# Block attention and a feed-forward product: weight scales by blocks, from sums of squares, with each weight tile fetched once

## The chip, the cores and the metric

The kernel runs on one core of a Trainium2 chip. The metric is the device time of one execution in microseconds, the median of several runs. A core has five engines that run side by side and wait for one another by semaphores: TensorE (PE, and PEld for its weight loads), VectorE (DVE), ScalarE (ACT), GpSimd (POOL) and SyncE (SP), which here issues all transfers.

## The reference

```python
def _attn_ref(q, k, v):                     # (4, 8, 768, 64) each
    block, window = (32, 16)
    k_sum = k.reshape(B, H, nb, block, D).max(axis=3)
    v_sum = v.reshape(B, H, nb, block, D).mean(axis=3)
    scores_l = scale * np.matmul(q, k.transpose(0, 1, 3, 2))     # kept where |i - j| < 16
    scores_s = scale * np.einsum('bhsd,bhnd->bhsn', q, k_sum) + np.log(block)
    ...                                                          # one softmax over both
    return np.matmul(a, v_all)

def _moe_ref(x, g_ln, w_ch1, w_ch2):        # x: (4, 768, 512)
    xn = (x - mu) / np.sqrt(var + 1e-06) * g_ln
    ch = np.maximum(xn @ w_ch1, 0.0) @ w_ch2                     # 512 -> 2048 -> 512
    return x + ch
```

The two weight matrices arrive as 64-bit floats, in pairs of 32-bit words: a low and a high one. The kernel takes 32-bit floats out of them by shifts and masks, and multiplies in 16-bit floats, each operand split in a high part and a rest (three matmuls for one product). So every weight tile is decoded, brought into the range of a 16-bit float by a power of two, and written as two 16-bit tiles.

## The kernel before, in words

The 3072 rows of x are 24 tiles T of 128 rows, six for each of four batches. Attention goes by steps t, two for a tile (four heads each). The 12 steps of the first batch (t < 12, the names early_...) work in 32-bit floats on data that is loaded whole; the later 36 work in split 16-bit floats, with the scales of their batch found from sums over the batch (`batch_k`, `batch_q`, `batch_v`, `batch_s`). After both steps of a tile stand its normalization (`ln`) and its transposition (`lnT`), into `xs`.

The feed-forward product goes by 12 groups g of two tiles, and by eight units in a group (`g1`, `g2` with s = 8 g + j). Unit j takes two of the 16 blocks of 128 hidden columns: `g1` makes h of them (24 matmuls of 256 columns into PSUM), ScalarE writes its positive part in 16 bits (hh), VectorE the rest (hl); `g2` multiplies both by the second matrix and adds to two accumulators a of 512 columns (12 matmuls). After unit 7 VectorE drains each accumulator, scaled, onto x, and SP writes it out. The accumulators of the second group lie in the PSUM pool that the attention uses for its products o.

The weights are 32 tiles of 128 x 512 values: 16 of the first matrix (i = 1) and 16 of the second (i = 2). `fetch_w` loads a raw tile (512 KB), `max_w` takes on VectorE the largest magnitude of each row's high words, `scale_w` makes of the 16 columns of a matrix one scale (a transposition, a reduction, a mask of the exponent, a matmul that spreads it to all rows), and `conv_w` decodes with three VectorE instructions into a temporary (wf; the buffers pta, ptb, mask), rescales on ScalarE into the high part and on VectorE into the rest (w). The first matrix' raw tiles stay where they are until they are converted. Those of the second go through a ring of four buffers, so they are fetched twice: once for the magnitude, once more to be converted.

The order on each engine is not that of the program text. A planner (`Plan`) records every instruction with its costs and dependences, schedules forward and backward for some rounds (`improve`), and issues the instructions sorted by the planned start. For the early stage its ranks are replaced by due times written by hand in `aim`, by stage: for example attention step t < 12 at 6 + 2.5 t us for the first four and at 14 + 9 t us for the others, and the other stages at 100 us or later. All engines run what is issued in that order, and so does SP's queue. All recorded instructions carry the same line number, that of the helper, so the profile is read by tile names.

Of the kernel before, what the change touches and what calls it, by code (L numbers as in the profile page):

```python
# [57 lines left out]


def aim(stage, found):  # L60


    if not stage:
        return found
    name, (t, *more) = stage[0], stage[1] or (0,)
    parts = ("early_k", "early_qk", "softmax", "early_transp", "early_pv")
    if name in parts and t < NEARLY:
        return (6 + 2.5 * t if t < 4 else 14 + 9 * t) + parts.index(name)
    if name in ("ln", "lnT") and t < NT:
        return (14 + 5 * t if t < 2 else 28 + 18 * t) + (name == "lnT")  # L70
    if name == "fetch_w":
        return (3 if t == 1 else 60 if len(more) > 1 else 30) + (5 if len(more) > 1 else 1.5) * more[0]
    if name == "max_w":
        return (10 if t == 1 else 34) + 1.5 * more[0]
    if name == "scale_w":
        return 36 if t == 1 else 60
    if name == "conv_w":
        n = more[0]
        return 38 + 3.2 * (n + n // 4 * 4 if t == 2 else n if n < 8 else n + n // 4 * 4 - 4) + 25.6 * (t == 2)
    if name in ("g1", "g2") and t < 16:  # L80
        return 0
    first = dict(fetch_k0=0, fetch_blocks=0.9, fetch_v0=1 + 0.1 * t, batch_k=3, batch_v0=5, gain=5, fetch_tail=5 * t)
    first["fetch_q"] = (0.5, 2)[t] if t < 2 else 15 + t
    if name in first and not (name == "batch_k" and t):
        return first[name]
    return max(found, 100)


class Plan:
# [207 lines left out]
    def issue(self, nc):  # L297
        after = [self.waits(x) for x in self.ops]
        then = [[] for _ in after]
        for i, x in enumerate(after):  # L300
            for j, wait in x:
                then[j].append((i, wait))
        rank = [0.0] * len(after)
        for i in reversed(range(len(after))):
# [4 lines left out]
        rank = [1e3 * aim(names[x.stage], t / 1e3) + 1e-4 * i for i, (x, t) in enumerate(zip(self.ops, start))]
        best = self.improve(rank, after, then, 2 * ROUNDS)  # L310
        self.time, self.start, self.end = best
        for _, i in sorted(zip(best[1], range(len(after)))):
            for op, a, k in self.ops[i].calls:
                getattr(getattr(nc, self.ops[i].engine), op)(*a, **k)  # L314
# [4 lines left out]
def body(ctx: ExitStack, tc, qt, qa, qe, kt, ks, va, vb, vs, g_ln, w1, w2, blocks, out):  # L319
# [169 lines left out]
    def batch_s(b):  # L489
# [294 lines left out]
    def max_w(i, n):
        if n == 0:
            wm[i] = work(f"wm{i}", f"wm{i}", [P, NF])
        nc.vector.tensor_reduce(
            wm[i][:, n : n + 1], raw[i, n].bitcast(F32)[:, :, 1], axis=AX.X, op=ALU.max, apply_absolute_value=True
        )

    @pl.step
    def scale_w(i):

        m, t = wm[i].bitcast(U32), work(f"wd{i}", f"wd{i}", [P, NF], U32)
        nc.vector.tensor_scalar(t[:], m[:], 3, 0x3FFFFFF8, ALU.logical_shift_left, ALU.bitwise_and)
        nc.vector.scalar_tensor_tensor(t[:], m[:], 0x40000000, t[:], ALU.bitwise_and, ALU.bitwise_or)
        x = t.bitcast(F32)
        if i == 1:
            x4 = x.rearrange("p (q c) -> p q c", c=4)
            nc.vector.tensor_tensor(x4, x4, gcol[:, 1:2].to_broadcast([P, 4, 4]), ALU.mult)  # L800
        mx = work(f"wx{i}", f"wx{i}", [P, 1])
        nc.vector.tensor_reduce(mx[:], x, axis=AX.X, op=ALU.max)
        ps = psum("hs"[i - 1], f"wps{i}", [P, 512])
        nc.tensor.transpose(ps[:1, :P], mx[:], ident[:])
        m1 = work(f"wy{i}", f"wy{i}", [1, 4])
        nc.vector.tensor_reduce(m1[:, 0:1], ps[:1, :P], axis=AX.X, op=ALU.max)
        nc.vector.tensor_scalar(m1[:, 0:1], m1[:, 0:1], 2.0**-30, None, ALU.max)
        mi = m1.bitcast(U32)
        nc.vector.tensor_scalar(mi[:, 3:4], mi[:, 0:1], 0x7F800000, 0x7F800000, ALU.bitwise_and, ALU.bitwise_and)
        nc.vector.tensor_scalar(mi[:, 1:2], mi[:, 3:4], 0x7F800000, 0x7F800000, ALU.bitwise_and, ALU.bitwise_xor)  # L810
        nc.vector.tensor_scalar(m1[:, 2:3], m1[:, 1:2], (W1TOP if i == 1 else W2TOP) / 4.0, None, ALU.mult)
        nc.tensor.matmul(ps[:, 128:130], ones1[:1], m1[:, 2:4], start=True, stop=True)
        sv = wsc[i] = work(f"ws{i}", f"ws{i}", [P, 6])
        nc.vector.tensor_copy(sv[:, :2], ps[:, 128:130])
        if i == 1:
            nc.vector.tensor_scalar(sv[:, 2:6], gcol[:, 0], sv[:, 0:1], None, ALU.mult)
        else:
            nc.vector.tensor_scalar(
                sv[:, 2:3], sv[:, 1:2], wsc[1][:, 1:2], 16.0 / (XSCALE * W1TOP * W2TOP) / 4.0, ALU.mult, ALU.mult
            )  # L820

    @pl.step
    def conv_w(i, n):

        lw, hw = raw[i, n][:, :, 0], raw[i, n][:, :, 1]
        x = work(("pta", "ptb", "mask")[n % 3], f"wf{i}_{n}", [P, DM], U32)
        nc.vector.tensor_scalar(x[:], hw, 3, 0x3FFFFFF8, ALU.logical_shift_left, ALU.bitwise_and)
        nc.vector.scalar_tensor_tensor(x[:], hw, 0xC0000000, x[:], ALU.bitwise_and, ALU.bitwise_or)  # L830
        nc.vector.scalar_tensor_tensor(x[:], lw, 29, x[:], ALU.logical_shift_right, ALU.bitwise_or)
        j, u = divmod(n, 2)
        if u == 0:
            pair[i, j] = work(f"w{j + 8 * (i - 1)}", f"w{i}_{j}", [P, 2, 2, DM], F16)
        w, xf = pair[i, j][:, u], x.bitcast(F32)
        sc = wsc[1][:, 2 + n % 4 : 3 + n % 4] if i == 1 else wsc[2][:, 0:1]
        nc.scalar.activation(w[:, 0], xf, AF.Copy, scale=sc)
        nc.vector.scalar_tensor_tensor(w[:, 1], xf, sc, w[:, 0], ALU.mult, ALU.subtract)
# [25 lines left out]
    def g2(s):  # L864
        g, j = divmod(s, 8)
        hh, hl = st["h", s]
        if j == 0:
# [4 lines left out]
        for i in range(2):
# [3 lines left out]
            for c, ps in enumerate(acc[i]):  # L876
                cs = slice(DM // parts * c, DM // parts * (c + 1))
                with pl.unit():
                    for u in range(2):
                        f = 2 * j + u  # L880
                        for n, (h, a) in enumerate(((hh, 0), (hh, 1), (hl, 0))):
# [4 lines left out]
                                start=(j == 0 and u == 0 and n == 0),  # L886
                                stop=(j == 7 and u == 1 and n == 2),
                            )
                if j == 7:
                    nc.vector.scalar_tensor_tensor(  # L890
                        xt[T][:, cs], ps[:, : DM // parts], wsc[2][:, 2:3], xt[T][:, cs], ALU.mult, ALU.add
                    )
# [62 lines left out]
    for n in range(NF):  # L955
        fetch_w(1, n)
        max_w(1, n)
    for n in range(NF):
        fetch_w(2, n)
        max_w(2, n)  # L960
# [98 lines left out]
```

## Time and profile before

| what | value |
| --- | --- |
| time, median of 3 runs | 675.01 us (674.98 to 677.14) |
| the profiled execution, its own time | 675.17 us |
| its span, first to last instruction | 673.4 us |
| PE, DVE, ACT, POOL busy | 622.6, 462.9, 369.9, 186.9 us |
| mean granted clock of TensorE | 0.957 |
| moved by transfers | 101.53 MB |

In the profile's rows a group is named by the tiles written and read (out<-in), with the count, the busy time, the mean time of one, and the idle time of the engine ahead of it with what ended it. Tiles of interest: raw (weights as they arrive), wm (largest magnitudes), wf (decoded), w (16-bit weights), h, hh, hl (first product), a (accumulators of the second), x (rows of the residual stream), p (scores), pT (transposed).

### The profile page before, as it was taken

The page shows a single profiled execution, that of the slowest core. Times are in us where ns is not written, and L with a number is a line of the kernel's source. Part 1 is how long each engine was busy: PE and PEld are TensorE (multiplying, and loading weights), DVE is VectorE, ACT ScalarE, POOL GpSimd, SP SyncE. Part 2 cuts the span into 40 slices and gives each one's busy share as a digit, 9 for nine tenths or more (in the row PEclk, how much of TensorE's full clock was granted, in tenths as well). Part 3 has the DMA queues.
Part 4 walks back from the last instruction along what each step waited for, and adds up shares of the span by engine and source line. Part 5 has one row for each costly group of instructions (what it writes and reads, how often), then busy time and mean ns, then how long its engine had stood idle before and what let it go on. Part 6 is the DMA issues. An engine that isn't in the chain of part 4 may idle for free.

```text
span 673.4 us, 13368 instructions
## 1 busy us (share of the span) xinstructions
PE 622.6 (92%) x4629; PEld 439.1 (65%) x4629; DVE 462.9 (69%) x1183; ACT 369.9 (55%) x970; POOL 186.9 (28%) x405
## 2 busy tenths in 40 slices
PE   8665678999899999997989999999999999999998
PEld 5544455766567677665657676667677676666676
DVE  4999989979647988767667877677767776431111
ACT  3653385775557776656757666566665756311010
POOL 4100211003223533344433434343333344300000
PEclk9958578999999999999989999999999999999999
DMA  9999335644577676657776664656566654310000
GB/s 312 407 336 329 145 107 175 214 147 77 174 177 175 161 185 149 150 150 159 188 163 150 146 166 127 125 147 142 130 139 133 147 118 108 63 33 17 17 16 32
DMA packets 127300, 101.53 MB, mean 151 GB/s; under 512 B 85120, under 2 KB 107648, under 8 KB 127232
## 3 DMA queue, kind: packets, MB, share of 16 engines
q1 hardware_dynamic: 127232, 100.68, 56.5%
q8 instruction: 36, 0.59, 0.4%
q14 instruction: 32, 0.26, 0.1%
HBM read 74.66 MB, written 6.29 MB: 120 GB/s over the span
## 4 chain that ended last, share of the span: by engine, by line
PE 53%; DMA 16%; DVE 15%; ACT 8%; issue 3%; SPq 3%; POOL 1%; ACTq 0%; POOLq 0%; DVEq 0%
PE h L314 23%; PE a L314 22%; DMA ksg<-in_kt 5%; DVE wf L314 3%; PE o L314 3%; PE s L314 3%; DMA bst<-in_qa 3%; ACT p L314 3%; SPq L314 3%; DMA pT<-p 2%; DVE wm L314 2%; DMA bst<-in_ks 2%; ACT kh L314 2%; DVE p L314 1%; DVE kl L314 1%
## 5 line engine op out<-in xcount | busy, mean ns | idle before, releaser
L314 PE MATMUL h<-xs,w 128*128 128x256 f16 x2304 | 282.7, 278 | 16.0 <-DVE hl L314 9.3
L314 PEld LDWEIGHTS <-w 128*128 128x128 f16 x2304 | 227.9, 100 | 63.5 <-issue 9.7
L314 PE MATMUL a<-w,hh 128*128 128x512 f16 (+1 forms) x768 | 225.5, 376 | 0.0
L314 PE MATMUL a<-w,hl 128*128 128x512 f16 (+1 forms) x384 | 144.2, 375 | 0.0
L314 PEld LDWEIGHTS <-hh 128*128 128x128 f16 x800 | 77.5, 98 | 61.7 <-issue 0.8
L314 DVE SCALAR_TENSOR_TENSOR hl<-h,hh 128x512 f16<-128x512 f32 x96 | 65.8, 686 | 70.6 <-ACT hh L314 70.0
L314 ACT ACTIVATE hh<-h 128x512 f16<-128x512 f32 x96 | 56.2, 586 | 86.7 <-PE h L314 70.2
L314 ACT ACTIVATE p<-p,mn,sv 128x184 f32<-128x184 f32 x144 | 76.0, 529 | 18.6 <-POOL mn L314 18.0
L314 POOL TENSOR_TENSOR p<-p,p 128x512 f16<-128x512 f32 x72 | 71.0, 996 | 28.5 <-ACT p L314 23.4
L314 DVE SCALAR_TENSOR_TENSOR kl<-ksg,sv,kh 128x368 f16<-128x368 f32 x72 | 49.7, 690 | 32.2 <-ACT kh L314 31.6
L314 PEld LDWEIGHTS <-hl 128*128 128x128 f16 x400 | 39.2, 98 | 44.8 <-DVE hl L314 0.9
L314 ACT ACTIVATE kh<-ksg,sv 128x368 f16<-128x368 f32 x72 | 43.0, 597 | 34.6 <-POOL ksg L314 34.4
L314 ACT ACTIVATE bst<-bst 128x384 f32<-128x384 f32 (+2 forms) x55 | 32.2, 586 | 46.1 <-DVE kmax L314 15.9
L314 DVE CUSTOM_DVE_ANT_0 p<-s,mask 128x184 f32<-128x184 f32 x144 | 42.2, 344 | 16.3 <-PE s L314 16.3
L314 POOL TENSOR_SCALAR mn<-mn,sv 128x2 f32<-128x2 f32 x72 | 26.5, 370 | 82.4 <-DVE mn L314 82.3
L314 POOL COPY ksg<-ksum 128x48 f32<-128x48 f32 x72 | 19.1, 265 | 104.7 <-DMA ksg<-in_kt 89.9
L314 DVE SCALAR_TENSOR_TENSOR v<-vst,sv,v 128x256 f16<-128x256 f32 x72 | 42.6, 613 | 3.2 <-ACT v L314 2.8
L314 ACT ACTIVATE qhl<-qs,sv 128x512 f16<-128x512 f32 x36 | 25.8, 717 | 28.6 <-PE s L314 22.6
L314 POOL TENSOR_TENSOR x<-x,rc 128x256 f32<-128x256 f32 x36 | 25.1, 698 | 35.4 <-DVE x L314 35.0
L314 ACT ACTIVATE w<-wf,ws 128x512 f16<-128x512 f32 x32 | 22.2, 716 | 21.1 <-DVE wf L314 21.0
L314 PE MATMUL o<-v,pT 128*128 128x128 f16 (+1 forms) x432 | 26.2, 211 | 8.2 <-DMA pT<-p 8.2
L314 ACT CAST p<-p 128x512 f16<-128x512 f32 x72 | 32.9, 503 | 0.1
(147 smaller groups left out, 762.1 us busy)
## 6 DMA issues: line engine op xcount, KB each, us to landing
raw<-in_w SPq DMA_DIRECT2D x32, 512.0 KB
ksg<-in_kt SPq DMA_DIRECT2D x72, 184.0 KB
qs<-in_qt SPq DMA_DIRECT2D x72, 128.0 KB
out_x<-x SPq DMA_DIRECT2D x23, 256.0 KB
vst<-in_va SPq DMA_DIRECT2D x36, 128.0 KB
bst<-in_ks SPq DMA_DIRECT2D x20, 192.0 KB
bst<-in_qa SPq DMA_DIRECT2D x15, 256.0 KB
bst<-in_vs SPq DMA_DIRECT2D x20, 192.0 KB
```

The lines of the kernel that those rows point to most:

```text
L314: getattr(getattr(nc, self.ops[i].engine), op)(*a, **k)
```

## The change

The weights are taken in one order, `SEQ`: eight tiles of the first matrix, eight of the second, eight of the first, eight of the second. The scales are one for each block of four tiles of the first matrix and one for each half (eight tiles) of the second. Each comes from the sum of squares of its tiles: `dec_w` decodes a tile with the three VectorE instructions, the last of which writes back over the raw tile's high words (step two words), then ScalarE squares it and sums by rows into a column of `wacc`. `scale_w` adds over rows with a matmul by ones, floors, takes the power -1/2 on GpSimd and masks the exponent. `conv_w` then rescales from the decoded tile. Each tile is fetched once; up to 16 raw tiles are held. The accumulators of the second product are drained after unit 3 and again after unit 7, since the two halves of the second matrix have scales of their own. `WORDER` puts the units of the first two groups behind the weights that they need. `aim` is gone: the planner's own ranks order the early stage too.

```diff
-XSCALE, W1TOP, W2TOP = 4.0, 16.0, 2.0**15
+XSCALE, W1TOP, W2TOP, SQ = 4.0, 2.0**9, 2.0**15, 2.0**-24
-ROUNDS = 24
+ROUNDS = 32
-LEAD = 2
+SEQ = [(1 + m // 8 % 2, m % 8 + m // 16 * 8) for m in range(2 * NF)]
+WBLOCK, WHALF = (0, 4, 16, 20), (8, 24)
+RAWS = [f"w{4 + m}" for m in range(12)] + [f"ring{m}" for m in range(4)]
+RAWS += [f"w{m}" for m in range(10, 16)] + ["ring0", "ring1"] + [f"w{m}" for m in range(12, 16)]
+RAWS += [f"ring{m}" for m in range(4)]
+AWAY = 24
+WORDER = (
+    ((1, 0), 0, 4, (), (0, 1)),
+    ((1, 1), 4, 4, (16, 17), (2, 3)),
+    ((2, 0), 8, 8, (18, 19, 20, 21, 22, 23), (8, 9, 10, 11)),
+    ((1, 2), 16, 4, (24, 25), (4, 5)),
+    ((1, 3), 20, 4, (26, 27, 28, 29, 30, 31), (12, 13, 6, 7, 14, 15)),
+    ((2, 1), 24, 8, (), ()),
+)
-def aim(stage, found):
...
-        start = self.improve(rank, after, then, ROUNDS)[1]
-        names = {n: k for k, n in self.stages.items()}
-        rank = [1e3 * aim(names[x.stage], t / 1e3) + 1e-4 * i for i, (x, t) in enumerate(zip(self.ops, start))]
-        best = self.improve(rank, after, then, 2 * ROUNDS)
+        best = self.improve(rank, after, then, ROUNDS)
...
-    def max_w(i, n):
...
-    def scale_w(i):
...
+    def fetch_w(m):
+        i, n = SEQ[m]
+        raw[m] = work(RAWS[m], f"raw{m}", [P, DM, 2], U32)
...
+    def dec_w(m):
+        i, n = SEQ[m]
+        lw, hw = raw[m][:, :, 0], raw[m][:, :, 1]
+        tmp = ("pta", "ptb", "mask")
+        x = work(tmp[m % 3 if m < AWAY else m % 2], f"wf{m}", [P, DM], U32)
         nc.vector.tensor_scalar(x[:], hw, 3, 0x3FFFFFF8, ALU.logical_shift_left, ALU.bitwise_and)
         nc.vector.scalar_tensor_tensor(x[:], hw, 0xC0000000, x[:], ALU.bitwise_and, ALU.bitwise_or)
-        nc.vector.scalar_tensor_tensor(x[:], lw, 29, x[:], ALU.logical_shift_right, ALU.bitwise_or)
+        y = work(tmp[2], f"wy{m}", [P, DM], U32)[:] if m == AWAY else hw
+        nc.vector.scalar_tensor_tensor(y, lw, 29, x[:], ALU.logical_shift_right, ALU.bitwise_or)
+        xf[m] = y.bitcast(F32)
+        nc.scalar.activation(
+            x.bitcast(F32), xf[m], AF.Square, scale=gcol[:, 1, n % 4 : n % 4 + 1] if i == 1 else SQ,
+            accum_out=wacc[:, m : m + 1],
+        )
+    def scale_w(i, k):
+        first, count = (WBLOCK[k], 4) if i == 1 else (WHALF[k], 8)
+        v = wv[:, 4 * (k + 4 * (i - 1)) :]
+        ps = psum("h", f"wps{i}_{k}", [P, 512])
+        nc.tensor.matmul(ps[:, :count], ones[:], wacc[:, first : first + count], start=True, stop=True)
+        nc.vector.tensor_reduce(v[:, 0:1], ps[:, :count], axis=AX.X, op=ALU.add)
+        nc.vector.tensor_scalar(v[:, 0:1], v[:, 0:1], 2.0**-100, None, ALU.max)
+        nc.gpsimd.tensor_tensor(v[:, 0:1], v[:, 0:1], mhalf[:], ALU.pow)
...
+    def conv_w(m):
...
+        sc = sc1[:, n : n + 1] if i == 1 else sc2[:, n // 4 : n // 4 + 1]
+        nc.scalar.activation(w[:, 0], xf[m], AF.Copy, scale=sc)
+        nc.vector.scalar_tensor_tensor(w[:, 1], xf[m], sc, w[:, 0], ALU.mult, ALU.subtract)
...
     def g2(s):
-        if j == 0:
-            st["acc", g] = [[psum("ao"[g == 1], f"a{g}_{i}", [P, DM])] for i in range(2)]
-            if g == NG - 1:
+        if j % 4 == 0:
+            st["acc", g] = [[psum("ao"[g == 1], f"a{g}_{j}_{i}", [P, DM])] for i in range(2)]
+            if (g, j) == (NG - 1, 4):
...
+                if j % 4 == 3:
+                    nc.vector.scalar_tensor_tensor(
+                        xt[T][:, cs], ps[:, : DM // parts], kout[:, j // 4 : j // 4 + 1], xt[T][:, cs], ALU.mult, ALU.add
+                    )
                 if j == 7:
-                    nc.vector.scalar_tensor_tensor(
-                        xt[T][:, cs], ps[:, : DM // parts], wsc[2][:, 2:3], xt[T][:, cs], ALU.mult, ALU.add
-                    )
                     nc.sync.dma_start(out[T * P : T * P + P, cs], xt[T][:, cs])
...
     def gain():
-        nc.scalar.activation(gcol[:, 1], gcol[:, 0], AF.Abs)
+        nc.scalar.activation(gcol[:, 1], gcol[:, 0], AF.Copy, scale=SQ)
...
-    for j in range(8 + LEAD):
-        for g, i in ((0, j), (1, j - LEAD)):
-            if 0 <= i < 8:
-                g1(8 * g + i)
-                g2(8 * g + i)
+    for m in range(16):
+        fetch_w(m)
+    for (i, k), first, count, more, units in WORDER:
+        for m in range(first, first + count):
+            dec_w(m)
+        scale_w(i, k)
+        for m in range(first, first + count):
+            conv_w(m)
+        for m in more:
+            fetch_w(m)
+        for u in units:
+            g1(u)
+        if i == 2:
+            for u in range(4 * k, 4 * k + 4):
+                g2(u)
+                g2(8 + u)
```

More of the change, by code (lines that the diff above doesn't have):

```diff
@@ L57, in block_means @@
     return m
-def aim(stage, found):
[L63 to L86, printed above, removed]
 class Plan:
@@ L338, in body @@
     vst = [cp.tile([P, 2, 4, D], F32, name=f"vst{i}") for i in range(2)]
-    ones1 = cp.tile([3, P], F32, name="ones1")
+    ones = cp.tile([P, P], F32, name="ones")
+    wacc = cp.tile([P, 2 * NF], F32, name="wacc")
+    wsc = cp.tile([P, 60], F32, name="wsc")
     make_identity(tc.nc, ident)
@@ L343, in body @@
     nc.gpsimd.memset(mhalf[:], -0.5)
-    nc.gpsimd.memset(ones1[:], 1.0)
+    nc.gpsimd.memset(ones[:], 1.0)
     blk = work("kh1", "blk", [P, 144])
@@ L502, in batch_s @@
         nc.vector.tensor_scalar(m1[:, 5:8], ident[:3, :3], m1[:, 1:2], 2.0**-14, ALU.mult, ALU.mult)
-        nc.tensor.matmul(ps[:, 128:134], ones1[:], m1[:, 2:8], start=True, stop=True)
+        nc.tensor.matmul(ps[:, 128:134], ones[:3], m1[:, 2:8], start=True, stop=True)
         sv = work("sv", f"sv{b}", [P, 10], F32, 2)
@@ L769, in lnT @@
         nc.vector.tensor_tensor(xl, ps[:], xh, ALU.subtract)
-    raw, pair, wm, wsc = {}, {}, {}, {}
+    raw, xf, pair = {}, {}, {}
     @pl.step
-    def fetch_w(i, n, again=False):
-        tag, bufs = (f"w{n}", 1) if i == 1 else ("ring", 4)
-        d = raw[i, n] = work(tag, f"raw{i}_{n}" + "b" * again, [P, DM, 2], U32, bufs)
+    def fetch_w(m):
+        i, n = SEQ[m]
+        raw[m] = work(RAWS[m], f"raw{m}", [P, DM, 2], U32)
         fq, c = divmod(n, 4)
         src = w1[c * P : c * P + P, fq * DM : fq * DM + DM] if i == 1 else w2[n * P : n * P + P]
-        nc.sync.dma_start(d[:], src.bitcast(U32).rearrange("p (x t) -> p x t", t=2))
+        nc.sync.dma_start(raw[m][:], src.bitcast(U32).rearrange("p (x t) -> p x t", t=2))
@@ L783, in max_w @@
     @pl.step
-    def max_w(i, n):
[L785 to L788, printed above, removed]
+    def dec_w(m):
[3 more added lines that the diff above has]
+        x = work(tmp[m % 3 if m < AWAY else m % 2], f"wf{m}", [P, DM], U32)
+        nc.vector.tensor_scalar(x[:], hw, 3, 0x3FFFFFF8, ALU.logical_shift_left, ALU.bitwise_and)
+        nc.vector.scalar_tensor_tensor(x[:], hw, 0xC0000000, x[:], ALU.bitwise_and, ALU.bitwise_or)
+        y = work(tmp[2], f"wy{m}", [P, DM], U32)[:] if m == AWAY else hw
[5 more added lines that the diff above has]
+        )
@@ new lines, in body @@
+    p1, q1, sc1, sc2, kout, wv = (wsc[:, a:b] for a, b in ((0, 4), (4, 8), (8, 24), (24, 28), (28, 30), (30, 54)))
+    @pl.step
+    def scale_w(i, k):
[6 more added lines that the diff above has]
+        nc.gpsimd.tensor_tensor(v[:, 0:1], v[:, 0:1], mhalf[:], ALU.pow)
+        bits = lambda x: x.bitcast(U32)
+        power = 0x7F800000
+        if i == 1:
+            nc.vector.tensor_scalar(bits(p1[:, k : k + 1]), bits(v[:, 0:1]), power, power, ALU.bitwise_and, ALU.bitwise_and)
+            nc.vector.tensor_scalar(
+                sc1[:, 4 * k : 4 * k + 4], gcol[:, 0], p1[:, k : k + 1], SQ * W1TOP, ALU.mult, ALU.mult
+            )
+            nc.vector.tensor_scalar(bits(q1[:, k : k + 1]), bits(v[:, 0:1]), power, power, ALU.bitwise_and, ALU.bitwise_xor)
+            return
+        nc.vector.tensor_reduce(v[:, 1:2], p1[:, 2 * k : 2 * k + 2], axis=AX.X, op=ALU.min)
+        nc.vector.tensor_scalar(bits(v[:, 2:3]), bits(v[:, 0:1]), power, power, ALU.bitwise_and, ALU.bitwise_and)
+        nc.vector.tensor_scalar(v[:, 2:3], v[:, 2:3], v[:, 1:2], None, ALU.mult)
+        nc.vector.tensor_scalar(
+            sc2[:, 2 * k : 2 * k + 2], q1[:, 2 * k : 2 * k + 2], v[:, 2:3], SQ * W2TOP / 2, ALU.mult, ALU.mult
+        )
+        nc.vector.tensor_scalar(bits(v[:, 3:4]), bits(v[:, 2:3]), power, power, ALU.bitwise_and, ALU.bitwise_xor)
+        nc.vector.tensor_scalar(
+            kout[:, k : k + 1], v[:, 3:4], 0.5 / (XSCALE * SQ * SQ * W1TOP * W2TOP), None, ALU.mult
@@ L789, in max_w @@
         )
     @pl.step
-    def scale_w(i):
[L794 to L819, printed above, removed]
-            )
@@ L822, in conv_w @@
[L822 to L830, printed above, removed]
-        nc.vector.scalar_tensor_tensor(x[:], lw, 29, x[:], ALU.logical_shift_right, ALU.bitwise_or)
-        j, u = divmod(n, 2)
-        if u == 0:
[L834 to L838, printed above, removed]
+    def conv_w(m):
+        i, n = SEQ[m]
+        j, u = divmod(m, 2)
+        if u == 0:
+            pair[j] = work(f"w{j}", f"wp{j}", [P, 2, 2, DM], F16)
+        w = pair[j][:, u]
+        sc = sc1[:, n : n + 1] if i == 1 else sc2[:, n // 4 : n // 4 + 1]
+        nc.scalar.activation(w[:, 0], xf[m], AF.Copy, scale=sc)
+        nc.vector.scalar_tensor_tensor(w[:, 1], xf[m], sc, w[:, 0], ALU.mult, ALU.subtract)
@@ L885, in g2 @@
                                 wt[2, f][:, a, cs],
[L886 to L888 removed]
+                                start=(j % 4 == 0 and u == 0 and n == 0),
+                                stop=(j % 4 == 3 and u == 1 and n == 2),
+                            )
+                if j % 4 == 3:
+                    nc.vector.scalar_tensor_tensor(
+                        xt[T][:, cs], ps[:, : DM // parts], kout[:, j // 4 : j // 4 + 1], xt[T][:, cs], ALU.mult, ALU.add
+                    )
                 if j == 7:
[L890 to L892 removed]
                     nc.sync.dma_start(out[T * P : T * P + P, cs], xt[T][:, cs])
@@ L954, in body @@
     gain()
[L955 to L960, printed above, removed]
     for hp in range(4):
```

7 lines of the change are left out of this document (removed).

## The prediction, made before the change was timed

> **What bounds the kernel now.** I read the page first, then the table of engine time by stage, then the chain of waits inside the early stage, and last the groups by shape, which give the price of one instruction.
>
> ```profile
> span 673.4 us, 13368 instructions
> PE 622.6 (92%) x4629; PEld 439.1 (65%) x4629; DVE 462.9 (69%) x1183; ACT 369.9 (55%) x970; POOL 186.9 (28%) x405
> PEclk9958578999999999999989999999999999999999
> ```
>
> TensorE is busy 92% of the span, but a busy share over the whole span mixes stages. The clock digits lie between 5 and 8 in the third to seventh slice (34 to 118 us): there TensorE works in fits and starts.
>
> The table by stage (columns: stretch, its length, busy time of PE, PEld, DVE, ACT, POOL, then granted clock, DMA share, GB/s):
>
> ```profile
> 17.00:40.00 23.00, 14.07 (x107) 11.79 (x107) 21.73 (x64) 11.73 (x41) 3.75 (x13) 0.82 1.03 402
> 40.00:105.00 65.00, 44.82 (x254) 33.47 (x255) 59.51 (x153) 37.56 (x112) 7.28 (x20) 0.68 0.60 206
> 105.00:157.00 52.00, 50.64 (x344) 33.99 (x342) 48.44 (x120) 35.23 (x106) 5.81 (x13) 0.98 0.53 169
> 157.00:200.00 43.00, 39.70 (x268) 26.35 (x267) 28.18 (x76) 23.44 (x60) 11.05 (x27) 0.96 0.68 161
> 200.00:360.00 160.00, 150.86 (x1206) 106.88 (x1204) 119.71 (x305) 107.39 (x277) 61.52 (x120) 0.99 0.69 163
> 360.00:674.00 314.00, 307.34 (x2383) 216.78 (x2381) 178.30 (x450) 147.64 (x358) 89.78 (x167) 1.00 0.44 101
> ```
>
> Two stages, two limits. From 17 to 157 us VectorE is busy 21.73 + 59.51 + 48.44 = 129.7 of 140 us (93%) and ScalarE 84.5 us (60%). After 200 us TensorE is busy 458.2 of 474 us: there the end is set by TensorE's work. How little the multiplications get done early, in the same table for the two accumulators alone (h is the first product, a the second):
>
> ```profile
> 40.00:105.00 65.00, 23.85 (x148) 3.42 (x5) 3.42 (x6) 0.68 0.60 206
> 105.00:157.00 52.00, 15.64 (x128) 4.14 (x6) 2.92 (x5) 0.98 0.53 169
> 105.00:157.00 52.00, 25.93 (x108) 0.00 (x0) 0.98 0.53 169
> 350.92 2.59 PE a L314 x12
> 353.51 2.62 PE h L314 x24
> ```
>
> The last two rows are pieces of the chain of waits at full clock: one h matmul takes 2.62/24 = 0.109 us, one a matmul 2.59/12 = 0.216 us. So the 148 of 40 to 105 us are 16 us of work in 65 us, and no a matmul ran before 105 us. The chain of waits inside 40 to 160 us says who holds them up:
>
> ```profile
> by line: DVE wf L314 16.3%; PE a L314 12.0%; PE h L314 11.6%; DVE w L314 7.3%; DVE wm L314 6.0%; PE s L314 4.7%; DMA raw<-in_w 4.5%; DVE p L314 3.7%; DMA qs<-in_vs 3.6%; PE o L314 3.2%; issue 2.5%; ACT w L314 2.4%; ACT qs L314 2.3%; DMA bst
> ```
>
> Decoding (wf), rescaling (w) and the largest magnitude (wm), all VectorE, are the largest block. The early stage is bound by VectorE; what is saved there while TensorE starves comes off the end.
>
> **The change part by part.** Prices, from the groups by shape (busy, mean ns of one, idle before); the first row is that of 17 to 157 us, the others are of the whole span:
>
> ```profile
> L314 DVE TENSOR_REDUCE wm<-raw 128x1 f32<-128x512 f32 x31 | 20.9, 679 | 1.4 <-DMA raw<-in_w 1.4
> L314 DVE SCALAR_TENSOR_TENSOR wf<-raw,wf 128x512 uint32<-128x512 uint32 x32 | 21.6, 685 | 0.0
> L314 DVE SCALAR_TENSOR_TENSOR w<-wf,ws,w 128x512 f16<-128x512 f32 x32 | 23.6, 749 | 1.6 <-ACT w L314 1.5
> L314 ACT ACTIVATE w<-wf,ws 128x512 f16<-128x512 f32 x32 | 22.2, 716 | 21.1 <-DVE wf L314 21.0
> L314 ACT ACTIVATE bst<-bst 128x512 f32<-128x512 f32 x15 | 9.4, 625 | 15.9 <-DMA bst<-in_qa 15.9
> L314 ACT ACTIVATION_READ_ACCUMULATOR bst<-bst 128x1 f32 x35 | 6.6, 187 | 0.0
> L314 DVE TENSOR_SCALAR sv<-sv 128x1 f32<-128x1 f32 x9 | 1.4, 177 | 0.1
> L314 DVE SCALAR_TENSOR_TENSOR x<-a,ws,x 128x512 f32<-128x512 f32 x23 | 17.1, 744 | 11.3 <-PE a L314 11.3
> L314 POOL TENSOR_TENSOR rs<-rs,mhalf 128x1 f32<-128x1 f32 x24 | 14.7, 616 | 1.3
> L314 PE MATMUL wps<-wy,ones 1*128 1x2 f32 x4 | 1.2, 358 | 1.6 <-DVE wy L314 1.5
> ```
>
> *VectorE, early.* Of the 32 reductions, 31 lie in this stretch: 31 x 0.679 = 21.1 us go. The 21 short instructions of the two old scale chains go, the 36 of six new chains come: 15 more x 0.177 = 2.7 us. The second product is now drained by halves, so four evictions more for the first two groups: 4 x 0.744 = 3.0 us. Sum: 129.7 - 21.1 + 2.7 + 3.0 = 114.3 us. Decoding keeps its three instructions a tile, the last now writing at a step of two words. No row shows such a write: below, a gain has no reason, since the work per element stays; above, twice the 0.685, 22 us in all. I take nothing, because wm reads at the same step and costs 0.679, as a dense instruction does.
>
> *ScalarE, early.* 32 squares come. The nearest are the absolute sums, 0.625 us without a per-row scale, and the copy with one, 0.716: 16 of each, 21.5 us, and 32 x 0.187 = 6.0 us to read the sums. 84.5 + 27.5 = 112 us. They read at the step of two words as well (bound: from nothing to twice, 21 us; I take nothing for the reason above).
>
> *How long the stage is then.* VectorE 114 and ScalarE 112: two engines equally loaded, where one led. With VectorE as full as now (93%) it lasts 123 us and ends at 140. But two engines that feed each other don't both reach 93%. The best stretches with both loaded:
>
> ```profile
> 85.00:102.00 17.00, 12.85 (x80) 9.78 (x80) 13.78 (x34) 14.53 (x48) 3.33 (x7) 0.80 0.42 121
> 119.00:136.00 17.00, 17.00 (x123) 11.88 (x122) 15.93 (x40) 12.82 (x39) 0.66 (x3) 1.00 0.63 195
> ```
>
> There the two together fill 28.3 and 28.8 of 34 us, 84%: (114 + 112) / (2 x 0.84) = 135 us, end at 152. With today's mean of both, 214/280 = 77%, it would be 148 us, end at 165. I take 145, between the first two: ScalarE's idle time now is mostly hunger (its copies waited 21.0 us for wf), no ceiling. The last conversion comes 12 us earlier.
>
> *When the first product starts.* First and last start of three tiles' instructions now (duration least/median/most in ns, then the starts in us), and the last eviction of the second group:
>
> ```profile
> L314 PE MATMUL h<-xs,w x2304: 269/273/422, 53.6 to 660.7; 128*128 128x256 f16 x192
> L314 PE MATMUL a<-w,hh x768: 272/379/634, 108.1 to 669.1; 128*128 128x512 f16 x184, 128*128 128x256 f16 x8
> L314 DVE SCALAR_TENSOR_TENSOR w<-wf,ws,w x32: 733/751/761, 47.2 to 156.9; 128x512 f16<-128x512 f32 x32
> 195.27 0.75 DVE L314 SCALAR_TENSOR_TENSOR x<-a,ws,x 128x512 f32<-128x512 f32 x1
> ```
>
> Now the scale waits for all 16 tiles of the first matrix and the h matmuls begin at 53.6 us; then four tiles suffice. The a matmuls begin at 108 us; then eight tiles of the second matrix suffice. TensorE gets work to fill the starved 40 to 105 us. At the last conversion it must still do the four units of the second half for both groups, 8 x 2.59 = 21 us; now it needs 38 us from there (156.9) to that eviction (195.3). So that eviction comes 12 to 29 us earlier. I count 2 us beyond the 12: attention of the second batch starts when VectorE lets it (its mask lies in a decoding buffer, its batch sums are VectorE's), not when TensorE is free.
>
> *The scale chain itself.* Matmul (0.36 us), sum, floor, power on GpSimd (0.616), exponent mask, product: 0.36 + 4 x 0.177 + 0.616 = 1.7 us, and I allow 3 with the hand-overs, six times. Hidden: decoding in place leaves sixteen tiles ready to be decoded meanwhile. Without that cover it costs 6 x 3 = 18 us. GpSimd has the room (28%), and the PE matmuls are 6 x 0.36 us.
>
> *Queues.*
>
> ```profile
> SPq L314 <- DVE wf L314: 22.5, 15, 5.2
> raw<-in_w SPq DMA_DIRECT2D x32, 512.0 KB
> raw_0b<-in_w SPq DMA_DIRECT2D x1, 512.0 KB
> ...
> raw_15b<-in_w SPq DMA_DIRECT2D x1, 512.0 KB
> ```
>
> The sixteen second fetches go, 8.4 MB. But SP still holds: fetches 16 to 31 wait for rescaled tiles (now 22.5 us of waiting for wf), and the loads of the next batch stand behind them. Worth between -2 and +2 us; I take nothing.
>
> *Later.* Twenty more evictions, 15 us of VectorE, which is 75% busy from 200 to 360 us and 57% after: hidden by that room. At each of 12 new borders TensorE must have its accumulator back; from nothing (no a matmul is shown waiting now) to 12 x 0.3 us. I take 1 us. The last group's split second accumulator begins half-way: pairs of 256-wide matmuls become 512-wide ones, the same columns, nothing. The gain's copy and the larger tile of ones replace like instructions ahead of the first weight: nothing.
>
> *The written order.* The hand-set due times go, and the planner's own ranks decide. No row prices it. Bounds: the planner already sets everything after 100 us, where TensorE is full; in the early stage a bad order can cost what the loads ahead cost. I take nothing and give it a rival.
>
> **Sum.** -12 - 2 + 1 = -13 us on the profiled execution of 675.2 us (span 673.4 and 1.8 around it); that stands 0.2 above the median, 675.0. Predicted: 662 us.
>
> **Rivals.**
>
> 1. *The lead of TensorE is kept whole.* The eviction of the second group comes up to 29 us earlier and nothing later gives it back. For: 49 of 65 us between 40 and 105 us hold no product. Against: after 200 us attention's loads end waits.
>
> ```profile
> POOL ksg L314 <- DMA ksg<-in_kt: 51.8, 21, 5.4
> ```
>
> (Waits of 200 to 360 us.) Price: 675 - 29 + 1 = 647 us.
>
> 2. *Attention of later tiles absorbs it.* That same row is the evidence for: if the late chain of load, scores, transposition and product doesn't move up by more than a few us, TensorE idles longer between 160 and 360 us. It would give 672 us, 675 at worst.
>
> 3. *Slower: ScalarE becomes the bound.* Each engine takes its instructions as they are written; a square that waits for a decode holds back the exponentials and the evictions of h behind it, and VectorE waits for one of three temporaries until the square has read. Place: 20 to 160 us. It decides when ScalarE can't be filled beyond 112/140 = 80% while VectorE works; the 119 to 136 us row has 75%, the 85 to 102 row 85%. At today's mean of the two the stage ends at 165, 8 us late: 683 us.
>
> 4. *Slower: the planner's order.* First loads of attention behind weight fetches, or the third and fourth tile of attention behind conversions so that the second group has no input. One full queue of sixteen fetches is 8.4 MB at 402 GB/s, 21 us; half of that is 685 us.
>
> 5. *Slower: squares need another table.*
>
> ```profile
> L314 ACT ACT_TABLE_LOAD x1 | 1.3, 1283 | 4.0 <-DMA k<-in_ks 4.0
> ```
>
> One load serves Exp, Abs, Relu and copies today. Were Square outside, each of the eight early attention steps from the fifth on would cost two loads: 8 x 2.57 = 20.5 us of ScalarE, 132 us; at 84% for both 147 us, end at 164, 682 us. The Trainium skill, ScalarE: Activation LUTs, Table sets: the hidden batching unit, tells to group calls by set and lists relu, copy, identity and abs as in every set, Square not among them. By that rule alone squares could bring reloads; the trace agrees for the four listed and shows no Square.
>
> **How the numbers follow.** My case (655 to 669) has 50%, rival 1 17%, rival 2 13% (8 of it still faster, 5 unchanged), rival 3 13%, rival 4 5%, rival 5 2%. A difference under 0.3%, 2 us, can't be told from none in this kernel. Faster: 50 + 17 + 8 = 75%; same 5%; slower 20%. The range reaches into rivals 1 and 3: 646 to 678 us leaves out some 8% below and 12% above.
>
> **What would show it.** The wm group is gone and 32 squares of 0.6 to 0.75 us stand on ScalarE; the first h matmul comes before 45 us, the first a matmul before 85; VectorE between 17 us and the last w falls to about 114 us, ScalarE rises to about 112; the last w comes at 140 to 152 us; the raw fetches number 32; TensorE's idle time after 200 us stays near 16 us. I am wrong if the last w comes after 157 us, if decode in place costs more than 0.75 us, if a second table load shows, or if TensorE idles in 160 to 360 us by as much more as it gained before.

## The result, and the profile after

| | before | after |
| --- | --- | --- |
| median, us | 676.0 (674.98 to 677.14, 4 runs) | 653.6 (652.11 to 661.02, 4 runs) |
| the profiled execution, us | 675.17 (span 673.4) | 652.65 (span 650.9) |

The ratio is 0.969, 95% interval 0.9613 to 0.9767: 3.1% faster. The prediction was 662 us, faster at 75%, range 646 to 678. One run of e3 below took 1062.3 us at a granted clock of 0.556, its three others 653 to 657 us at 0.979 to 0.982; it counts as slow, and all ratios are of fast runs.

The page of the kernel after, its first lines and the clock:

```profile
span 650.9 us, 13424 instructions
PE 617.9 (95%) x4611; PEld 436.1 (67%) x4611; DVE 455.7 (70%) x1190; ACT 392.2 (60%) x1034; POOL 195.7 (30%) x411
PEclk9957799999999999999999999999999999999999
```

The slices with a low clock were five and are three. The table by stage, with the stretches of before (columns as there):

```profile
17.00:40.00 23.00, 17.41 (x136) 14.14 (x134) 21.35 (x86) 20.49 (x75) 5.51 (x20) 0.91 1.02 386
40.00:105.00 65.00, 57.45 (x369) 45.85 (x370) 58.82 (x153) 57.11 (x170) 9.53 (x28) 0.77 0.40 128
105.00:157.00 52.00, 50.34 (x365) 35.22 (x362) 48.52 (x127) 41.05 (x112) 13.24 (x23) 1.00 0.52 156
157.00:200.00 43.00, 42.20 (x321) 28.05 (x319) 34.38 (x91) 32.02 (x84) 18.71 (x35) 1.00 0.85 211
200.00:360.00 160.00, 151.82 (x1195) 106.25 (x1192) 121.36 (x313) 106.26 (x273) 61.15 (x117) 1.00 0.70 164
360.00:651.00 291.00, 283.99 (x2168) 197.18 (x2167) 165.94 (x412) 129.48 (x309) 80.27 (x147) 1.00 0.39 94
```

TensorE runs 369 matmuls from 40 to 105 us where it ran 254, and the granted clock there is 0.77 where it was 0.68. VectorE is as full as ever (58.82 of 65 us, before 59.51); ScalarE went from 37.56 to 57.11. After 200 us TensorE is idle 8.2 + 7.0 = 15.2 us, before 15.8: nothing was gained or lost there. It is busy 151.82 + 283.99 = 435.8 us after 200 us, before 458.2: 22.4 us less work is left, as much as the whole gain.

Part of the early stage's gain goes with the clock. One h matmul took 23.85/148 = 0.161 us there before and takes 26.32/192 = 0.137 now, for 0.109 at full clock:

```profile
40.00:105.00 65.00, 26.32 (x192) 5.42 (x8) 4.77 (x8) 0.77 0.40 128
```

Whether the clock rose because TensorE worked more steadily, or TensorE did more because the clock rose, no run separates.

So the time was won before 200 us. What it was made of, the two products say. For each kernel the stretch from 0 to 200 us, h first, then a; the kernel before in the first two rows, the one after in the last two:

```profile
0.00:200.00 200.00, 59.27 (x429) 11.69 (x17) 9.83 (x17) 0.86 0.68 218
0.00:200.00 200.00, 45.34 (x192) 2.98 (x4) 0.86 0.68 218
0.00:200.00 200.00, 65.79 (x528) 14.23 (x21) 12.41 (x22) 0.91 0.64 198
0.00:200.00 200.00, 52.66 (x228) 5.84 (x8) 0.91 0.64 198
```

At 0.109 and 0.216 us, 99 h and 36 a matmuls more are 10.8 + 7.8 = 18.6 us of work done ahead; the rest of the 22.4 us, some 4 at this price, is other matmuls, those of attention. The later attention is ahead too. First and last start of the scores of the later batches, before and after, then of the transposed inputs of the product:

```profile
L314 DVE CUSTOM_DVE_ANT_0 p<-s,mask x144: 327/344/350, 175.7 to 577.3; 128x184 f32<-128x184 f32 x144
L297 DVE CUSTOM_DVE_ANT_0 p<-s,mask x144: 327/344/351, 150.2 to 545.5; 128x184 f32<-128x184 f32 x144
L314 SPq DMA_TRANSPOSE xs<-x x20: 1232/1242/2368, 162.8 to 594.6; - x20
L297 SPq DMA_TRANSPOSE xs<-x x20: 1232/1236/1811, 154.0 to 574.8; - x20
```

The scores start 25.5 us earlier and the first of these transposed inputs comes 8.8 us earlier, so I read it that TensorE's lead meets inputs that are there. The chain of waits from 40 to 105 us, before and then after:

```profile
by line: DVE wf L314 24.7%; DVE wm L314 11.1%; DVE w L314 10.3%; DMA raw<-in_w 8.4%; PE h L314 6.9%; DVE p L314 5.0%; PE s L314 4.8%; DMA bst<-in_qa 4.1%; ACT w L314 3.9%; DVE hl L314 2.8%; issue 2.7%; ACT p L314 2.6%; ACT qs L314 2.2%; ACT
by line: PE h L297 17.5%; ACT p L297 8.1%; DVE wf L297 8.0%; DVE raw L297 6.5%; PE o L297 5.2%; PE s L297 4.9%; issue 4.6%; ACT wf L297 4.5%; DMA bst<-in_vs 4.3%; DVE kmax L297 4.3%; ACT wp L297 3.9%; ACT hh L297 3.9%; PE pp L297 3.3%; DVE 
```

Decoding, rescaling and magnitudes on VectorE and the weights' transfers were 54.5% of it. Now no one engine leads: added up by engine, VectorE had 39 us of these 65 and has 19, as ScalarE has, and TensorE has 20.

### The profile page after: what moved, and what is told of

Same layout as the page of the kernel before. It is cut to its first block, busy times and chain, and to the rows that moved or that the text cites. A ratio compares the mean times of both kernels' runs of the same rounds, so it can differ in the third digit from the quotient of the medians.

```text
span 650.9 us, 13424 instructions
## 1 busy us (share of the span) xinstructions
PE 617.9 (95%) x4611; PEld 436.1 (67%) x4611; DVE 455.7 (70%) x1190; ACT 392.2 (60%) x1034; POOL 195.7 (30%) x411
## 4 chain that ended last, share of the span: by engine, by line
PE 40%; DMA 20%; DVE 19%; ACT 11%; issue 5%; POOL 2%; SPq 2%; ACTq 0%; POOLq 0%; DVEq 0%
PE a L297 17%; PE h L297 17%; DMA ksg<-in_kt 5%; ACT p L297 5%; DMA bst<-in_vs 4%; DMA bst<-in_ks 3%; PE o L297 3%; DMA pT<-p 3%; PE s L297 2%; DVE hl L297 2%; DVE x L297 2%; DVE kl L297 2%; DVE wf L297 2%; DVE p L297 2%; SPq L297 2%
## 5 line engine op out<-in xcount | busy, mean ns | idle before, releaser
L297 PE MATMUL h<-xs,wp 128*128 128x256 f16 x2304 | 277.6, 275 | 0.6 <-DVE hl L297 0.5
L297 PEld LDWEIGHTS <-wp 128*128 128x128 f16 x2304 | 226.1, 99 | 47.5 <-DVE hl L297 1.4
L297 PE MATMUL a<-wp,hh 128*128 128x512 f16 (+1 forms) x768 | 226.6, 377 | 0.0
L297 PE MATMUL a<-wp,hl 128*128 128x512 f16 x384 | 144.8, 377 | 0.0
L297 PEld LDWEIGHTS <-hh 128*128 128x128 f16 x784 | 75.4, 98 | 60.6 <-issue 0.2
L297 DVE SCALAR_TENSOR_TENSOR kl<-ksg,sv,kh 128x368 f16<-128x368 f32 x72 | 46.7, 648 | 27.9 <-ACT kh L297 27.5
L297 POOL COPY ksg<-ksum 128x48 f32<-128x48 f32 x72 | 20.9, 290 | 90.2 <-DMA ksg<-in_kt 71.4
L297 DVE SCALAR_TENSOR_TENSOR x<-a,wsc,x 128x512 f32<-128x512 f32 (+1 forms) x48 | 35.3, 738 | 16.0 <-PE a L297 16.0
L297 DVE TENSOR_REDUCE x<-o 128x256 f32<-128x512 f32 x36 | 24.6, 685 | 11.9 <-PE o L297 9.5
```

## The experiments

The theory (V): VectorE's time bounds the early stage, and its saved reductions carry the gain. The rivals: the barrier (B), that is, no product before all tiles of a matrix have been reduced; the hand-set order (O); the second fetch; ScalarE as the next bound. The granted clock, which moves with them, is a rival that no experiment holds fixed. "Planned anew" means that the planner made a new order; e2, e3 and e4 keep the order of their parent. The runs of before beside each group had medians of 675.5 to 678.1 us.

**e1, the kernel before without its due times.**

```diff
-        start = self.improve(rank, after, then, ROUNDS)[1]
-        names = {n: k for k, n in self.stages.items()}
-        rank = [1e3 * aim(names[x.stage], t / 1e3) + 1e-4 * i for i, (x, t) in enumerate(zip(self.ops, start))]
-        best = self.improve(rank, after, then, 2 * ROUNDS)
+        best = self.improve(rank, after, then, 3 * ROUNDS)
```

> The kernel before, its hand-set due times taken out; the planner's own ranks order everything. Theory V (VectorE's saved reductions and the earlier product carry the 22 us): the order carries little, 668 to 690 us. Rival O (the change gained because the hand-set order went): at or under 662 us.

678.93 us, ratio 1.0017 (0.9992 to 1.0043). The order by hand was worth nothing that can be told; rival O falls. Here the later scores start at 160.4 us, 15 us before those of the kernel before, and nothing is gained by that alone.

**e2 and e5, the kernel before without the reductions' time**: left out in the same order, with a constant in their columns, then planned anew over 8 of 512 columns. The constant is there from the start, so in e2 only the fixed order still keeps the product behind the scale; in e5 the data do too. e5 also lowers `W2TOP` to 2.0**13.

```diff
 e2: in issue
+                if not k.get("apply_absolute_value"):
...
 e5: in max_w
-            wm[i][:, n : n + 1], raw[i, n].bitcast(F32)[:, :, 1], axis=AX.X, op=ALU.max, apply_absolute_value=True
+            wm[i][:, n : n + 1], raw[i, n].bitcast(F32)[:, :8, 1], axis=AX.X, op=ALU.max, apply_absolute_value=True
```

> The kernel before in its own order; the 32 largest-magnitude reductions are left out and a constant stands in their columns. All fetches and the two barriers of the scales stay. Theory V (VectorE's time by itself): 21.5 us less VectorE work in a stage that it fills to 93%, so 658 to 664 us. Rival B (the barrier: the product can't start before all weights of a matrix have been read and reduced; VectorE's time is filled by nothing else meanwhile): 668 us or more, first h matmul still after 48 us.

> The kernel before, planned anew, its 32 reductions over 8 of the 512 columns only (the scale is that of these columns): VectorE is spared some 19 us and the planner knows it; fetches and barriers stay. If the reductions left out earlier brought little (5 us) because that kernel's order was fixed: 655 to 664 us here. If the barrier keeps VectorE's saved time from being used: 668 to 673 us again.

e2: 671.56 us, ratio 0.9916 (0.9882 to 0.9949). e5: 668.65 us, 0.9892 (0.9853 to 0.993). Some 19 to 21 us of VectorE taken out bring 6 to 7 us, and a new order doesn't change that: theory V had asked for 658 to 664 us of e2. From e2, the stretch from 17 to 40 us, and VectorE's longest wait in it:

```profile
17.00:40.00 23.00, 14.56 (x113) 12.17 (x112) 14.69 (x54) 12.16 (x43) 3.81 (x14) 0.83 1.03 400
DVE x L315 <- PE o L315: 2.9, 4, 1.0
```

VectorE now stands idle 8.3 of these 23 us, before 1.3: it waits for the early attention's products and scores, and nothing fills these gaps, for in this order the first rescaling comes at 46.3 us.

**e6, the kernel before without the barrier**: constant scales (`csc`), planned anew; all reductions and fetches stay.

```diff
-        sc = wsc[1][:, 2 + n % 4 : 3 + n % 4] if i == 1 else wsc[2][:, 0:1]
+        sc = csc[:, n % 4 : n % 4 + 1] if i == 1 else csc[:, 4:5]
...
```

> The kernel before, planned anew, with constant scales: nobody waits for the largest magnitudes, all reductions and all three fetches stay (their result is not read). Theory B (the barrier withholds the product): first h matmul before 45 us and 655 to 666 us. Theory V (VectorE's work is what counts): 670 to 677 us, for the work is the same.

668.48 us, ratio 0.9897 (0.9857 to 0.9937). The first h matmul starts at 44.8 us:

```profile
L314 PE MATMUL h<-xs,w x2304: 272/273/421, 44.8 to 652.7; 128*128 128x256 f16 x192
40.00:105.00 65.00, 45.18 (x280) 34.22 (x281) 62.77 (x162) 34.41 (x98) 9.15 (x21) 0.78 0.59 199
```

The barrier alone is worth 7 us as well, and the time falls between what the two theories had asked for. VectorE, which still does the reductions, is 97% full from 40 to 105 us.

**e9, both out: constant scales and small reductions; e10, the second matrix also fetched once.** e9 joins the edits of e5 and e6. e10 adds:

```diff
-    for n in range(NF):
-        fetch_w(2, n)
-        max_w(2, n)
...
             if i == 2:
-                fetch_w(2, n, True)
+                fetch_w(2, n)
+                max_w(2, n)
             conv_w(i, n)
```

> The kernel before, planned anew, with constant scales and with the reductions over 8 of 512 columns: barrier and reductions are both out, all three fetches stay. Each alone brought 7 us. If they are two halves of one effect (VectorE's order of work ahead of the product): 661 us, 14 less. If each only needs the other out of the way: 655 us or less. If they are the same 7 us: 666 to 669 us.

> As the run before, and the second matrix fetched once only (through its ring of four, ahead of its conversion): what then is missing of the change is the order of the tiles, the 16 raw buffers and the two accumulators a group. If the second fetch costs nothing: as the run before within 3 us. If the transfers count: 4 to 10 us less.

Both are planned anew; e10 also has its reductions behind the fetches that stay. e9: 660.66 us, ratio 0.9759 (0.9711 to 0.9806), about the sum of the two. e10: 654.15 us, 0.9652 (0.96 to 0.9703), 6.5 us less again, and as fast as the changed kernel, with constant scales but without its order of tiles, its 16 raw buffers and its halved evictions. From 40 to 105 us, the stage of e9 and of e10, then the h matmuls of each:

```profile
40.00:105.00 65.00, 56.17 (x347) 41.83 (x347) 62.80 (x173) 36.93 (x100) 8.71 (x18) 0.81 0.71 244
40.00:105.00 65.00, 56.39 (x398) 41.89 (x397) 62.30 (x166) 40.12 (x117) 10.37 (x24) 0.92 0.31 104
40.00:105.00 65.00, 27.73 (x183) 4.78 (x7) 4.19 (x7) 0.81 0.71 244
40.00:105.00 65.00, 27.79 (x208) 5.42 (x8) 4.69 (x8) 0.92 0.31 104
```

VectorE does the same 62 us in both; the transfers fall from 71% to 31% of their engines and 51 matmuls more get done. TensorE's busy time is the same (56.17 and 56.39 us): an h matmul takes 0.134 us where it took 0.152, at a granted clock of 0.92 instead of 0.81. How fewer fetches come to raise the clock was not tested. Three parts, then, of about 7 us each: reductions, barrier, second fetch. Each stands on one plan or two, and e11 below shows that another plan by itself can go with 3 us.

**e7, the changed kernel with scales from eight tiles of the first matrix**, planned anew.

```diff
-    ((1, 0), 0, 4, (), (0, 1)),
-    ((1, 1), 4, 4, (16, 17), (2, 3)),
+    ((1, 0), 0, 8, (16, 17), (0, 1, 2, 3)),
...
-    ((1, 2), 16, 4, (24, 25), (4, 5)),
-    ((1, 3), 20, 4, (26, 27, 28, 29, 30, 31), (12, 13, 6, 7, 14, 15)),
+    ((1, 2), 16, 8, (24, 25, 26, 27, 28, 29, 30, 31), (4, 5, 12, 13, 6, 7, 14, 15)),
...
-        first, count = (WBLOCK[k], 4) if i == 1 else (WHALF[k], 8)
+        first, count = ((0, 0, 16, 16) if i == 1 else WHALF)[k], 8
...
```

> The changed kernel, planned anew, with the first matrix' scales from eight tiles at a time in place of four; all work is the same. Theory B: the product starts later and 3 to 10 us come back, 657 to 664 us. Theory V: 652 to 656 us.

656.88 us, ratio 0.9723 (0.969 to 0.9757), just between what the two theories had asked for; the changed kernel's interval covers it. Blocks of four are not shown to be better than of eight.

**e11, the changed kernel from 31 planning rounds.**

> The changed kernel with one planning round less (31 for 32): the same work, perhaps in another order. It tells how much a plan by itself moves the time: 652 to 657 us expected; differences of that size between kernels planned anew prove nothing.

656.49 us, ratio 0.9702 (0.9651 to 0.9754), runs from 653.65 to 660.78. The same work in another order: the 3 to 4 us by which e7 and e8 (below) stand above the changed kernel are no more than another plan goes with by itself.

**e8, drained four times a group**, planned anew.

```diff
-        if j % 4 == 0:
+        if j % 2 == 0:
...
-                if j % 4 == 3:
+                if j % 2 == 1:
```

> The changed kernel, planned anew, its accumulators drained four times a group in place of twice: 48 evictions more, 36 us of VectorE, and 24 borders more at which TensorE needs its accumulator back. If evictions by halves are nearly free, as forecast (1 us for 24): 653 to 658 us. If they cost 0.3 us a border or more, or VectorE's room is gone: 661 us or more.

657.68 us, ratio 0.9731 (0.9697 to 0.9766). Forty-eight evictions and 24 borders more go with 4 us by the medians and 1 us against e11's plan, so the 24 evictions of the change are not shown to cost anything.

**e4, the reductions put back into the changed kernel, same order; e3, its squares left out, same order.**

```diff
 e4: behind the third decoding instruction
+                if len(a) > 4 and a[4] == ALU.logical_shift_right:
+                    n = self.extra = getattr(self, "extra", -1) + 1
+                    nc.vector.tensor_reduce(
+                        self.spare[:, n : n + 1], a[0].bitcast(F32), axis=AX.X, op=ALU.max, apply_absolute_value=True
+                    )
...
 e3: in issue
+                if op != "activation" or a[2] != AF.Square:
```

> The changed kernel in its own order, with a reduction to the largest magnitude (read by nothing) behind each decode: 32 x 0.68 = 21.8 us of VectorE come back, nothing else. Theory V: 664 to 674 us. Rival B or O: under 658 us.

> The changed kernel in its own order; the 32 squares are left out, their sums are a constant; the scale chains stay. ScalarE is 85% busy from 17 to 157 us with them. If ScalarE is a second bound: 636 to 646 us. If its squares lie beside VectorE's work: 649 us or more.

e4: 670.09 us, ratio 0.9893 (0.9848 to 0.9938), some 14 us of the gain gone for 21.8 us of VectorE. From 17 to 157 us it is 97% busy, and TensorE runs 789 matmuls where the changed kernel runs 865 (e4, then the changed kernel):

```profile
17.00:157.00 140.00, 111.59 (x789) 85.89 (x785) 135.52 (x361) 108.92 (x328) 21.05 (x58) 0.89 0.51 171
17.00:157.00 140.00, 125.21 (x865) 95.21 (x864) 128.70 (x364) 118.65 (x353) 28.28 (x71) 0.88 0.55 181
```

e3: 653.5 us, the median of three, 0.9665 (0.9614 to 0.9716). In this order the squares cost nothing that can be told; a new plan without them was not tried. The 14 us are an upper price for the reductions: the fixed order could not make room for them.

**e12, the changed kernel with two decoding instructions a tile**, planned anew. The low words' three bits are left out.

```diff
-        nc.vector.scalar_tensor_tensor(x[:], hw, 0xC0000000, x[:], ALU.bitwise_and, ALU.bitwise_or)
...
-        nc.vector.scalar_tensor_tensor(y, lw, 29, x[:], ALU.logical_shift_right, ALU.bitwise_or)
+        nc.vector.scalar_tensor_tensor(y, hw, 0xC0000000, x[:], ALU.bitwise_and, ALU.bitwise_or)
```

> The changed kernel, planned anew, with two VectorE instructions a tile to decode in place of three: the three bits of the low words are left out, so the weights are cut to 21 bits. 32 x 0.685 = 21.9 us of VectorE less. Theory V: 632 to 642 us, as much gained as the added reductions lost. If ScalarE (85% busy from 17 to 157 us) is by now the bound: 646 us or more.

655.46 us, ratio 0.968 (0.964 to 0.9721): nothing, where theory V asked for 632 to 642. Three views of e12: the stage, the first a matmul (89.1 us in the changed kernel), the first later scores (150.2 there):

```profile
17.00:157.00 140.00, 123.65 (x879) 91.01 (x878) 116.80 (x344) 121.59 (x365) 30.05 (x76) 0.93 0.59 192
L297 PE MATMUL a<-wp,hh x768: 272/379/379, 74.8 to 649.2; 128*128 128x512 f16 x188, 128*128 128x256 f16 x4
L297 DVE CUSTOM_DVE_ANT_0 p<-s,mask x144: 315/344/351, 147.1 to 547.2; 128x184 f32<-128x184 f32 x144
```

VectorE has 12 us more room, the second product starts 14 us earlier, and yet the later scores start only 3 us earlier and end 2 us later. The early lead, 18 a matmuls or 3.9 us at 105 us, is given back: at 200 us e12 has 538 h and 228 a matmuls done, the changed kernel 528 and 228, and after that its TensorE is busy as long (435.1 us, for 435.8) and idle 3 us longer.

```profile
0.00:200.00 200.00, 66.47 (x538) 14.38 (x21) 12.65 (x22) 0.95 0.65 200
0.00:200.00 200.00, 53.09 (x228) 5.94 (x8) 0.95 0.65 200
200.00:360.00 160.00, 150.32 (x1194) 105.46 (x1192) 124.96 (x320) 106.49 (x275) 62.79 (x123) 1.00 0.67 164
360.00:654.00 294.00, 284.77 (x2163) 197.54 (x2161) 160.43 (x400) 126.50 (x301) 79.21 (x143) 1.00 0.39 92
```

As a bound on its own VectorE is thus used up by the change. What holds the changed kernel now is open: in its own order ScalarE alone it isn't (e3), VectorE alone neither. In e12 ScalarE is busy 121.59 of the 140 us, so with VectorE relieved it may be the bound, as the expectation allowed. That the later attention's start holds it is a reading of e12's rows, and e1 shows that an earlier start by itself can bring nothing; both engines relieved together, or that attention started earlier by itself, was not tried. No version among these is shown to beat the changed kernel.

## Why the prediction was right or wrong

*That VectorE's early stage starves TensorE, and that the time comes off there:* right. All of the 22.5 us between the two profiled executions was won before 200 us; TensorE's idle time afterwards was to stay near 16 us and is 15.2. How much of it is the higher clock of that stage is open.

*The size, 13 us:* too small. One term came out by luck, one failed, and one that I had put at nothing was not nothing.

- *"The last conversion comes 12 us earlier."* It comes later, at 162.1 us for 156.9. Conversions, and then the last eviction of the second group, which stood at 195.27 us before:

```profile
L297 DVE SCALAR_TENSOR_TENSOR wp<-raw,wsc,wp x31: 719/746/1548, 41.4 to 162.1; 128x512 f16<-128x512 f32 x31
182.80 0.74 DVE L297 SCALAR_TENSOR_TENSOR x<-a,wsc,x 128x512 f32<-128x512 f32 x1
```

  That eviction comes 12.5 us earlier all the same, because only 20.7 us of work are left after the last conversion (my 21) instead of 38.4. So the amount of 12 was right by luck: it came from the shorter tail and not from an earlier conversion. VectorE's early work was to fall to 114 us and is 128.7, for other work moved in: 16 instructions of hl in this stretch where there were 11, and the second batch's first k, q and scores. The last raw tile is fetched only at 126.2 us; whether the planner or the buffers kept it back was not tested. The test that I had named, a last w after 157 us, was a bad one: it looked at the producer's last item and not at what TensorE had done by then.
- *"I count 2 us beyond the 12."* This is the step that failed: it is 10 us. I held that attention of the second batch would not follow TensorE. Its scores start 25.5 us earlier, and TensorE's lead of 18.6 us of products at 200 us is kept to the end. The lead is work on the third group: 528 h and 228 a matmuls are 22 and 19 units, where the first two groups have 16 and the kernel before had done 18 and 16. So rival 1, which had 17%, is right in that nothing later gives the lead back, and wrong in that the second group ends 12.5 us earlier and not 29. Rival 2, the lead absorbed, didn't happen here, though e12 looks like it. My reason was the mask in a decoding buffer, and the change itself (`AWAY`) keeps the last tiles' decoding out of that buffer after tile 24: the mask was made after the last conversion and is now made before it. How much of the 25.5 us this brings, no run isolates.

```profile
L314 POOL TENSOR_SCALAR mask<-msk,sv x3: 725/725/727, 165.2 to 447.9; 128x552 f32<-128x552 f32 x3
L297 POOL TENSOR_SCALAR mask<-msk,sv x3: 981/1148/1205, 148.6 to 416.6; 128x552 f32<-128x552 f32 x3
```

- *The second fetch, "between -2 and +2 us, I take nothing".* e10 against e9 puts it at 6.5 us in the kernel before. The 8.4 MB stood in the same starved window, where the transfers were 60% busy. I had priced the queue; what came in its place is told by the granted clock (0.81 to 0.92), and its cause stays open.

*The reductions as the main term:* in part. In the kernel before, alone, they bring 6 to 7 us (e2, e5), not the 12 of the sum; the barrier, which I had in the prose and gave no term of its own, brings as much (e6).

*Right in their price:* the last decode in place, 0.682 us for a forecast 0.685; the squares hidden beside VectorE's work (e3), though they cost 0.777 and 0.671 us for 0.716 and 0.625; the evictions by halves (e8); the dropped hand order (e1), so that rival 4 fell. The first scale chain took from 36.9 to 39.7 us, 2.8 for an allowed 3. The squares' groups, and the first and the last step of that chain:

```profile
L297 ACT ACTIVATE wf<-raw,gcol 128x512 f32<-128x512 f32 x16 | 12.4, 777 | 0.9 <-ACT qs L297 0.6 <-DVE raw L297 0.2
L297 ACT ACTIVATE wf<-raw 128x512 f32<-128x512 f32 x15 | 10.0, 671 | 7.6 <-DVE vm L297 3.4 <-DVE raw L297 2.2 <-ACT bst L297 1.1
...
36.88 0.43 PE L297 MATMUL wps<-wacc,ones 128*128 128x4 f32 x2
...
39.50 0.22 DVE L297 TENSOR_SCALAR wsc<-gcol,wsc 128x4 f32<-128x4 f32 x1
```

*The two engines together:* an end at 145 us stands for a common fill of 226/256 = 88%, above the 84% of the rows that I had shown; they reach (128.7 + 118.65)/280 = 88%, but on 247 us of work, not 226. Rival 3 put the turning point at ScalarE being filled over 80%; it is filled to 85%. The first products came later than I named (h at 49.0 for under 45, a at 89.1 for under 85), and the gain was larger all the same.

*Rival 5, another table:* fell.

```profile
L297 ACT ACT_TABLE_LOAD x1 | 1.3, 1283 | 6.5 <-DMA k<-in_ks 6.5
```

One load, as before, with squares between the exponentials. The Trainium skill, ScalarE activation tables: per-element evaluation and per-set limits, What a function is on this engine, says that two functions of one set need no switch; the trace agrees with that for squares beside Exp, Abs, Relu and copies. The prediction let its trace agree for four listed functions; identity, the fourth, is not called in this kernel.

## What to carry to other kernels

When one engine starves another, measure a change by the work that the starved engine still has to do at a fixed time later, not by when the feeding engine's last item is out: freed time is filled with other work. Count all of that work. e9 has done the same 528 h and 228 a matmuls at 200 us as the changed kernel and is 8.8 us slower in its profiled execution, for with attention's matmuls TensorE is still busy 150.83 + 290.47 = 441.3 us, not 435.8:

```profile
200.00:360.00 160.00, 150.83 (x1187) 105.75 (x1185) 117.68 (x304) 108.71 (x279) 61.85 (x120) 0.99 0.69 166
360.00:660.00 300.00, 290.47 (x2235) 204.43 (x2232) 166.04 (x422) 136.54 (x329) 86.84 (x155) 0.99 0.42 99
```

Reductions and barrier brought 7 us each, alone; together they brought their sum, and the second fetch on top 6.5 more. And the same engine's time can have two prices: 21.8 us of VectorE put back cost 14 us, 21.9 us more taken out gave none.

## What the runs showed of the hardware that was not expected

ScalarE took longer on the decoded tile in place, at a step of two words, than on a dense one, while VectorE did not: the rescaling copy's mean is 0.763 us for 0.716 before. VectorE's reading and writing at that step stayed at 0.682.

```profile
L297 ACT ACTIVATE wp<-raw,wsc 128x512 f16<-128x512 f32 x31 | 22.6, 763 | 1.3 <-DVE wsc L297 1.3
L297 DVE SCALAR_TENSOR_TENSOR raw<-raw,wf 128x512 uint32<-128x512 uint32 x31 | 20.8, 682 | 0.0
L297 POOL TENSOR_TENSOR wsc<-wsc,mhalf 128x1 f32<-128x1 f32 x6 | 5.0, 840 | 20.8 <-DVE wsc L297 20.8
```

Whether the step or a busier memory makes the 0.047 us was not separated. For the step speaks the one tile that is decoded into a dense buffer: its copy took 0.705 us and its square 0.627, where the tiles in place took 0.763 and 0.671; e4, e8, e11 and e12 show the same, 0.705 to 0.706 for 0.754 to 0.757. The power on GpSimd took 0.840 us in the mean of six, for 0.616 in the mean of the normalizations before.
